# Second level of the 7-for-8 algorithm for all seven outer products of the last block's last product

## Chip, cores, metric

One core of a Trainium2 chip. The metric is the device time of one execution in microseconds (us), the median over runs.

## The reference

Attention with normalised q and k, then a bilinear feed-forward. The change touches the last line's second product only.

```python
# q, k, v: (8, 12, 448, 64); x: (3584, 768) after the heads are laid side by side
def _moe_ref(x, w_a, w_b, w_out):          # w_a, w_b: (768, 1536); w_out: (1536, 768)
    a = x @ w_a
    b = x @ w_b
    return (a * b @ w_out).astype(np.float32)
```

## The kernel before

The 3584 rows are taken in four blocks of 896 (`NB` is 4). Each block has two stages after attention: quarter products (`x @ w_a`, `x @ w_b`) and the last product (`@ w_out`). In both, a product of 2 x 2 quarters is done with seven products for eight; these seven are "product 0" to "product 6", issued in the order 0, 1, 2, 4, 3, 5, 6. In the last product, a product can be done plainly, tile by tile (128 tokens x 768 rows x 384 columns: six matmuls), or a pair of tiles can be split by the same scheme again: seven inner products of three matmuls with 192 columns each. That is the second level. It needs sums of the left factor's quarters (`Si`, four per pair, VectorE), sums of the right factor's quarters (`ti`, made once in an earlier block, kept in DRAM and fetched, four tiles per product), and more additions.

```python
        TWICE = {NB - 2: (0, 1, 2, 3, 4, 5, 6), NB - 1: (1, 2, 3, 4, 6)}   # block: products with a second level
        ...
            def each(f, a, base, to):
                twice = groups if f in TWICE.get(beta, ()) else []
                for t in pairs if not twice else alone:
                    product(t, f, a(t), plain(t, base, to))          # L726: 6 matmuls of 384 columns
                for g in twice:
                    inner_products(beta, key + place_of[f], f, g, a, base, to, acc, (c_, U_), out_place)
        ...   # groups is [(0, 1), (2, 3)] in the last block: no tile is left alone
            each(0, lambda t: A(0, 0, t), None, 0)
            for t in pairs:
                sum_(A(0, 0, t), A(0, 0, t), A(1, 0, t), ALU.subtract)
            each(1, n_, 0, 1)
            each(2, lambda t: A(0, 1, t), 0, (0, 0))
            for t in pairs:
                sum_(A(0, 1, t), A(0, 1, t), n_(t), ALU.subtract)
                sum_(n_(t), A(1, 0, t), A(1, 1, t), ALU.add)
            each(4, n_, 1, 0)
            ...
        # inside inner_products (L901 is its matmul); cut
            direct = base is None or (quarters and len(to) > 2)      # true for products 0 and 5 only
            product("a", a00, b_quarter(0, 0), nx0 + [st], True, False)
            product("b", s(1), b_made(1), ...)
            product("a", a01, b_quarter(1, 0), nx0 + [st], False, True)
            product("d", s(0), b_made(0), ...)
            product("g", s(2), b_made(2), ..., True, False)
            if not direct:                                            # two sums ahead of the read of g
                add(0.3, ...)                                         # L954
                add(0.55, ...)                                        # L955
            add(0.36, ... held["g"] ...)                              # L957: reads g before g goes on
            third()                                                   # "e"
            product("g", a11, b_made(3), ..., False, True)
```

A planner in the kernel orders all instructions beforehand from estimated durations.

In the profile lines, PE is TensorE, DVE VectorE, ACT ScalarE, POOL GpSimd and SP SyncE. `hT` holds the hidden rows (the left factor), `fin` sums of them and the running results, `st` the right factor; `Si` are the inner sums of the left factor, `ti` those of the right; `po` and `a`, `b`, `d`, `e`, `g`, `h` are PSUM banks, `pi` partial results, `oi` and `o_sb` output tiles. A line number can move by some lines in an edited kernel (L901 becomes L902).

## Time and profile before

| | |
|---|---|
| time, first three runs | 1550.15 us (1547.28 to 1551.54) |
| TensorE busy | 97%, granted clock 0.999 |
| last block's last product | 1438.38 to 1542.39, 104.0 us |
| after the last matmul | 6.2 us: one addition, then the stores |

How to read it: TensorE is never without work for long, so what shortens its queue shortens the kernel; the prediction shows the lines. The page's chain of what ended last says the same by each engine's share of the span:

```profile
PE 82%; DMA 7%; DVE 5%; ACT 3%; issue 1%; POOL 1%; SPq 1%; ACTq 0%; DVEq 0%; POOLq 0%
```

### The profile page before, as it was taken

To read this page: it belongs to the slowest core of one execution; us is meant where nothing else is said; L and a number is where in the kernel's file an instruction comes from. 1 tells how busy PE (TensorE), PEld (TensorE's weight loads), DVE (VectorE), ACT (ScalarE), POOL (GpSimd) and SP (SyncE) were. 2 spreads that over 40 slices of the span, in tenths; PEclk is the share of its full clock that TensorE was granted. 3 is DMA by queue.
4 is the path that set the end of the run, shared out by engine and by line. 5 is a ranking of instruction groups with operands and counts; after the bars stand their busy time and mean duration, and the time that the engine had idled before them with its cause. 6 is when DMAs were issued, how large, how long until landed. Compare 5 with 4: busy or idle time off the path is not lost.

```text
span 1548.6 us, 18051 instructions
## 1 busy us (share of the span) xinstructions
PE 1506.9 (97%) x6996; PEld 822.6 (53%) x6996; DVE 813.7 (53%) x1179; ACT 400.7 (26%) x654; POOL 314.1 (20%) x166
## 2 busy tenths in 40 slices
PE   8988999999999999999999999999999999999998
PEld 5553345555444555555444455555547855555796
DVE  5877869888786412222587543222237622222583
ACT  6767661111567100000445500000041000000000
POOL 3426432111345200011244300000111001000000
PEclk9999999999999999999999999999999999999999
DMA  9897445644445542212345456121226742222343
GB/s 269 240 268 199 97 108 178 218 163 175 143 118 128 150 146 76 103 71 107 102 110 152 114 159 199 72 107 71 95 83 206 247 159 100 79 82 91 111 140 110
DMA packets 128866, 214.74 MB, mean 139 GB/s; under 512 B 57860, under 2 KB 108292, under 8 KB 119044
## 3 DMA queue, kind: packets, MB, share of 16 engines
q1 hardware_dynamic: 100708, 160.02, 35.0%
q10 hardware_dynamic: 28064, 53.48, 9.9%
q8 instruction: 57, 0.93, 0.2%
q14 instruction: 37, 0.30, 0.1%
HBM read 169.08 MB, written 44.21 MB: 138 GB/s over the span
## 4 chain that ended last, share of the span: by engine, by line
PE 82%; DMA 7%; DVE 5%; ACT 3%; issue 1%; POOL 1%; SPq 1%; ACTq 0%; DVEq 0%; POOLq 0%
PE pq L1003 48%; PE po L726 16%; PE sc L515 5%; PE o L537 4%; DMA q_sb<-in_q_dram 2%; PE g L901 2%; PE a L901 2%; ACT ET L521 2%; PE pt L494 2%; DMA rec<-inv 1%; PE b L901 1%; PE su L573 1%; PE e L901 1%; PE d L901 1%; DMA lraw<-in_moe_w_b_dram 1%
## 5 line engine op out<-in xcount | busy, mean ns | idle before, releaser
L1003 PE MATMUL pq<-x,st 128*128 128x448 f32 x2016 | 763.5, 540 | 0.9 <-ACT rec L586 0.9
L1003 PEld LDWEIGHTS pq<-x,st 128*128 128x128 f32 x2016 | 381.2, 190 | 379.5 <-issue 371.2
L521 ACT ACTIVATE ET<-sc,ms 128x448 f32<-128x448 f32 x336 | 191.7, 633 | 92.2 <-PE sc L515 65.6
L515 PE MATMUL sc<-qkT 64*64 64x448 f32 x1344 | 177.2, 544 | 18.0 <-ACT ET L521 10.6
L537 PE MATMUL o<-ET,v_sb 64*64 64x448 f32 x1344 | 187.2, 545 | 7.5 <-ACT ET L521 6.9
L464 POOL TENSOR_TENSOR ms<-ms,expo 128x14 f32<-128x14 f32 x48 | 145.6, 3037 | 188.3 <-DVE ms L462 187.6
L1051 POOL TENSOR_TENSOR hT<-hT,t 128x448 f32<-128x448 f32 x24 | 28.4, 1185 | 744.7 <-DVE t L1049 742.5
L726 PE MATMUL po<-st,hT 128*128 128x384 f32 x504 | 166.4, 487 | 0.0
L726 PEld LDWEIGHTS po<-st,hT 128*128 128x128 f32 x504 | 95.0, 190 | 67.9 <-issue 3.9
L551 POOL TENSOR_TENSOR sum<-sum,ET 128x896 f32<-128x896 f32 x38 | 81.4, 2141 | 139.1 <-ACT ET L521 97.0
L1025 ACT COPY hT<-pq 128x448 f32<-128x448 f32 x24 | 12.8, 532 | 372.9 <-PE pq L1003 372.9
L515 PEld LDWEIGHTS sc<-qkT 64*64 64x64 f32 x1344 | 58.1, 132 | 95.2 <-issue 34.8
L537 PEld LDWEIGHTS o<-ET,v_sb 64*64 64x64 f32 x1344 | 60.2, 132 | 87.9 <-ACT ET L521 42.2
L726 PE MATMUL po<-st,fin 128*128 128x384 f32 x264 | 89.9, 490 | 0.0
L551 DVE TENSOR_TENSOR sum<-sum,ET 128x896 f32<-128x896 f32 x57 | 62.8, 1101 | 26.6 <-POOL sum L551 19.4
L726 PEld LDWEIGHTS po<-st,fin 128*128 128x128 f32 x264 | 49.1, 190 | 39.0 <-issue 7.0
L1063 POOL TENSOR_TENSOR hT<-hT,t 128x448 f32<-128x448 f32 x48 | 58.5, 1219 | 53.7 <-DVE t L1060 45.5
L458 DVE TENSOR_REDUCE ms<-sq 128x14 f32<-128x896 f32 x48 | 51.8, 1079 | 27.7 <-ACT sq L456 27.5
L1056 DVE TENSOR_TENSOR hT<-U,pq 128x448 f32<-128x448 f32 x48 | 29.8, 621 | 66.5 <-PE pq L1003 66.5
L746 DVE TENSOR_TENSOR o_sb<-fin,po 128x384 f32<-128x384 f32 x36 | 20.0, 554 | 80.2 <-PE po L726 72.4
L1060 DVE TENSOR_TENSOR t<-U,pq 128x448 f32<-128x448 f32 x48 | 29.7, 619 | 59.6 <-PE pq L1003 57.3
L1028 ACT COPY t<-pq 128x448 f32<-128x448 f32 x24 | 12.8, 533 | 176.0 <-PE pq L1003 176.0
(117 smaller groups left out, 1297.0 us busy)
## 6 DMA issues: line engine op xcount, KB each, us to landing
st<-kept SPq DMA_DIRECT2D x36, 1344.0 KB
st<-kept_o SPq DMA_DIRECT2D x28, 1152.0 KB
kept<-st ACTq DMA_DIRECT2D x12, 1344.0 KB
ti<-kept_t SPq DMA_DIRECT2D x48, 288.0 KB
q_sb<-in_q_dram SPq DMA_DIRECT2D x48, 224.0 KB
k_sb<-in_k_dram SPq DMA_DIRECT2D x48, 224.0 KB
v_sb<-in_v_dram SPq DMA_DIRECT2D x48, 224.0 KB
rec<-inv SPq DMA_DIRECT2D x48, 224.0 KB
```

The source lines that it names most:

```text
L458: op("DVE", 1.1, key, lambda: nc.vector.tensor_reduce(rs[p][:, s], xs["sq", nm, p], AX, ALU.add), [sq], [f"{ms}/{nm}"])
L464: lambda: nc.gpsimd.tensor_tensor(msf(), msf(), expo[:, 0:2 * NT * (b - a)], ALU.pow), [], names)
L494: nc.tensor.transpose(t[:, j * P:(j + 1) * P], x[:, j].rearrange("p h d -> p (h d)"), ident)
L515: nc.tensor.matmul(t[low_high[w], e, 0:S], lhsT=qkTs[p][low_high[e], 1, j * P + w * D:j * P + (w + 1) * D], rhs=qkTs[p][low_high[e], 0, w ...
L521: nc.scalar.activation(E[:, e], scs[p, j][:, e, 0:S], AF.Exp, scale=rs[p][:, 1, 2 * j + e:2 * j + e + 1])
L537: nc.tensor.matmul(os_[p][low_high[e], w, 0:S], lhsT=xs["v", p][low_high[w], e, j * D:(j + 1) * D], rhs=ETs[p, j][low_high[w], e], start=( ...
L551: two[e].tensor_tensor(sums[p], sums[p] if j > 1 else ETs[p, 0], ETs[p, j], ALU.add)
L726: nc.tensor.matmul(held["po"][:, 0:HALF], lhsT=a[0]()[:, c], rhs=sts[beta, 12 + place_of[f]][:, c], start=(c == 0), stop=(c == MH - 1))
L901: nc.tensor.matmul(held[bank], lhsT=x()[:, c], rhs=y(c), start=(start and c == 0), stop=(stop and c == MI - 1), skip_group_check=True)
L1003: nc.tensor.matmul(banks[bank][:, 0:S], lhsT=sts[at][:, f, c * P:(c + 1) * P], rhs=quads[x][:, c], start=(start and c == 0), stop=(stop an ...
L1056: take("DVE", 0.68, lambda bank=bank, i=i, n=n: V.tensor_tensor(C(i, n), held["U"], PS(bank), ALU.add), [f"p{ident_}.{bank}", U], [hp[i]])
L1063: lambda i=i, n=n, nm=nm: two[TIMES].tensor_tensor(C(i, n), C(i, n), held[nm], ALU.mult), [t], [hp[i]],
```

## The change

The two products that the kernel before leaves plain in the last block, 0 and 5, get the second level too: fewer matmul columns, for more sums and fetches.

```diff
-        TWICE = {NB - 2: (0, 1, 2, 3, 4, 5, 6), NB - 1: (1, 2, 3, 4, 6)}
+        TWICE = {NB - 2: (0, 1, 2, 3, 4, 5, 6), NB - 1: (0, 1, 2, 3, 4, 5, 6)}
```

## The prediction

> **What bounds the kernel now.** I read the page's head first (who is busy), then the timeline of TensorE over the last block's last product (the stage that the change touches), then the table of stretches for that stage, then the waits inside it, and last the same stage of the block before, where all seven outer products already use the second level.
>
> ```profile
> span 1548.6 us, 18051 instructions
> PE 1506.9 (97%) x6996; PEld 822.6 (53%) x6996; DVE 813.7 (53%) x1179; ACT 400.7 (26%) x654; POOL 314.1 (20%) x166
> PEclk9999999999999999999999999999999999999999
> ...
> 1438.38 11.77 PE L726 MATMUL po<-st,hT 128*128 128x384 f32 x36
> 1449.99 4.03 PE L726 MATMUL po<-st,fin 128*128 128x384 f32 x12
> 1453.86 1.14 PE L901 MATMUL a<-st,fin 128*128 128x192 f32 x6
> 1454.83 1.14 PE L901 MATMUL b<-ti,Si 128*128 128x192 f32 x6
> ...
> 1459.82 1.24 PE L901 MATMUL g<-ti,fin 128*128 128x192 f32 x6
> 1460.89 1.14 PE L901 MATMUL a<-st,fin 128*128 128x192 f32 x6
> ...
> 1485.24 1.24 PE L901 MATMUL b<-ti,Si 128*128 128x192 f32 x6 [1.80 <-DVE Si L877]
> ...
> 1512.50 11.77 PE L726 MATMUL po<-st,hT 128*128 128x384 f32 x36
> 1524.11 4.03 PE L726 MATMUL po<-st,fin 128*128 128x384 f32 x12
> 1527.98 1.14 PE L901 MATMUL a<-st,hT 128*128 128x192 f32 x6
> 1529.26 1.24 PE L901 MATMUL b<-ti,Si 128*128 128x192 f32 x6
> ```
>
> TensorE is 97% busy at full clock, and in this stage it has almost no gap, so the stage is as long as its matmuls. The stage runs from 1438.38 to 1542.40. Its seven outer products stand in the order 0, 1, 2, 4, 3, 5, 6. The two plain ones, 0 and 5, are the L726 rows: 48 instructions in 15.48 us each (1438.38 to 1453.86, 1512.50 to 1527.98), so 0.3225 us per instruction. The other five are L901: an inner product of six instructions comes every 0.975 us (1454.83 less 1453.86), 0.1625 us per instruction. A busy figure would mislead, as ends overlap; I go by start-to-start distances.
>
> ```profile
> 1438.38:1453.86 15.48, 15.48 (x50) 9.12 (x48) 9.07 (x16) 1.43 (x3) 1.13 (x1) 1.00 0.23 78
> 1453.86:1467.93 14.07, 14.07 (x85) 13.59 (x84) 9.11 (x22) 1.12 (x3) 0.00 (x0) 1.00 0.44 136
> ...
> 1482.30:1498.43 16.13, 14.33 (x85) 13.56 (x85) 13.77 (x32) 0.64 (x2) 0.00 (x0) 1.00 0.38 130
> ...
> 1512.50:1527.98 15.48, 15.48 (x50) 9.12 (x49) 4.57 (x10) 0.00 (x0) 0.00 (x0) 1.00 0.54 169
> ```
>
> The columns are length, PE, PEld, DVE, ACT, POOL, clock, DMA share and GB/s. A plain product is 15.48 us long, a two-level one 14.07 when nothing is late. VectorE and the DMA engines have room in both plain ones.
>
> **What the Trainium skill says.** "TensorE: Matmul & The Clock Gate", section "Wait — 56ns, not 53.3ns?", puts warm matmuls start to start at N / 2.4 GHz plus about 2.5 ns: 82.5 ns for 192 columns, 162.5 for 384. The trace has 162.5 and 322.5 ns, twice that within 2%, as if each f32 instruction passed its columns twice; so time follows columns, and halving them costs no visible extra here. "VectorE: DVE Perf Modes", section "The TRN2 errata", gives (N+151)/0.96 for an fp32 tensor_tensor: 557 ns for 384, 357 for 192; the trace has 554 and about 352, so it agrees. "SBUF — State Buffer", section "Who interferes with whom", says that a VectorE instruction with two SBUF inputs contends with a GpSimd instruction that reads SBUF. In the block before, one such 384-wide sum beside a GpSimd multiply took 1.49 us in place of 0.55, which fits.
>
> **The change part by part.** A plain product handles four token tiles with 4 x 6 matmuls of 384 columns, each two instructions: 48. Two-level, they go as two groups of two tiles; a group is 7 inner products of 3 matmuls of 192 columns: 42 instructions. A group therefore costs at least 7 x 0.975 = 6.83 us against 24 x 0.3225 = 7.74 us. The four new groups can give at most 4 x 0.91 = 3.7 us: the whole prize is 0.24% of the time.
> Groups seen now take 7.03 (1453.86 to 1460.89), 0.2 over 6.83: the last inner product adds into a bank that VectorE must first read, and that read comes after two sums of 0.36 and 0.56 with the earlier accumulator. Products 0 and 5 take the code's direct form, which does not put those two sums ahead. Product 5 of the block before shows it:
>
> ```profile
> 1233.57 1.14 PE L901 MATMUL g<-ti,Si 128*128 128x192 f32 x6
> 1234.55 1.14 PE L901 MATMUL e<-st,Si 128*128 128x192 f32 x6
> 1235.52 1.14 PE L901 MATMUL g<-ti,hT 128*128 128x192 f32 x6
> ```
>
> No gap before the last g, so I use 6.83 for direct groups.
> - Product 0: 15.48 becomes 2 x 6.83 + 0.1 for restarting after a wait = 13.75; saves 1.7.
> - Product 5: 15.48 becomes 13.65 + 0.15; saves 1.7.
> - Product 6 starts now with a hole: its a at 1527.98, its b only at 1529.26, 1.28 later in place of 0.975, because b needs the PSUM bank that VectorE is still reading twice for product 5. Two-level product 5 reads its banks in 0.35 us pieces, so this 0.3 goes.
> - VectorE gains, per group, four sums of 0.554 and five additions of 0.352 = 4.0 us, and in product 5 four more of 0.556 (total 6.2, against 6.83 of TensorE). It loses eight additions of 0.55 in product 5; ScalarE's four copies of 0.48 in product 0 become eight of 0.32. Net some 16 us more of VectorE work, all beside matmuls if it is in time.
> - DMA gains 8 loads of 288 KB, 2.3 MB. The block before moved 280 GB/s in one product, so about 8 us of transfer, estimated, in stretches with shares 0.23 to 0.54. The first four can be fetched during the quarter products, into the buffers that product 2's now take then; product 2's own are to be fetched in the 14 us of product 1. The factors themselves are already made for all seven.
> Sum: 1.7 + 1.7 + 0.3 = 3.7 us gained on the path, before new waits. Nothing changes after the last product (6.2 us of additions and stores), which moves earlier whole.
>
> **The rivals.**
> (1) A wait at the start of product 0 takes its place. Its sums need the last of the hidden rows; no plain tile stands in front, as one does in the block before. Product a needs no sum; b needs two. In the trace the additions that finish the rows run at 1436.33 and 1438.65 on VectorE, GpSimd's multiply for the needed rows ends at 1438.16. If the first sum slips in between (as it does in the block before), the second ends near 1439.95, and b could start at 1440.0 in place of 1439.36: 0.65 late. If the scheduler puts d, which needs one sum, ahead of b, the wait is nil; working through its rule by hand, I get a, d, b, a, which speaks for nil. With both sums after the second addition it would be 1.1. Against a large loss: product 4 has the worst such wait and it is 1.8.
> (2) VectorE becomes the bound around product 5. At 6.2 of 6.83 us it is 91% full, and the tail of product 5's second group (2.9 us) plus the sums of product 6's second group (2.2) plus product 6's own additions (3.0) make 8.1 us in a 7.03 us group. The sums are not needed until the next group, so I expect 0 to 0.5 of lateness at product 6's bank read. That whoever tuned this left out exactly the two direct products speaks for this or (1). The 1.5 us stall in product 6 of the block before looks like this rival, but VectorE waits there for a store to release its buffer, and nine such buffers are free in the last block.
> (3) Loads late: product 2's at 2.3 MB (with its factors) in about 14 us need 164 GB/s; 280 was reached. I give it little; it would cost 1 to 3 us.
> If (1) and (2) both come in full, the gain shrinks to about 2; with (3) too, the time stays where it is or rises by 1. If none comes, it is 1546.4.
>
> **Range and chances.** I take 0.8 us off the 3.7 for (1) and (2), so 2.9 us: 1550.15 - 2.9 = 1547.2. The three runs of before alone spread over 4.3 us, more than the gain, so the range is set by that spread as much as by the rivals: 1544.6 to 1549.9. Leaving the 2% band would take 31 us, eight times the whole prize: within 2% 0.985, slower 0.01 (a stuck load or a disturbed run), faster 0.005.
>
> **What would show each step right or wrong.** In the changed kernel the timeline should have no L726 rows for the last block; its products 0 and 5 should be about 13.7 to 14.3 us long; a direct group 6.83 to 6.95. The stage from its first product to the last matmul should be 100.3 to 101.6 us in place of 104.0. VectorE's busy time should rise by about 16 us. Rival 1 is a wait on the Si sums of L877 before the first b; rival 2 a wait on L957 before a g in product 5 or 6, with VectorE without idle time there; rival 3 a wait on ti or st. Wrong would be: a direct group over 7.1 us, product 4's wait grown well past 1.8 us by the longer queue on VectorE, or the schedule of the quarter products altered, which I take to be untouched.

## The result, and the profile after

Six runs each: 1544.53 us (1542.72 to 1547.83) against 1549.8 us for the kernel before. The ratio, 0.9971 with a 95% interval of 0.9957 to 0.9985, is the mean time of one kernel's fast runs over that of the other's of the same rounds, so not quite the ratio of the two medians. The time is within 2%, as expected; the median lies 0.07 us under the low end of the predicted range.

The page's head and TensorE's timeline of the stage, for the kernel after:

```profile
span 1544.2 us, 18272 instructions
PE 1503.3 (97%) x7068; PEld 832.2 (54%) x7068; DVE 824.4 (53%) x1215; ACT 401.9 (26%) x658; POOL 314.6 (20%) x166
...
1437.78 1.14 PE L901 MATMUL a<-st,hT 128*128 128x192 f32 x6
1439.19 1.24 PE L901 MATMUL b<-ti,Si 128*128 128x192 f32 x6 [0.28 <-DVE Si L877]
...
1445.15 1.14 PE L901 MATMUL a<-st,hT 128*128 128x192 f32 x6
...
1451.97 1.14 PE L901 MATMUL a<-st,fin 128*128 128x192 f32 x6
...
1483.33 1.24 PE L901 MATMUL b<-ti,Si 128*128 128x192 f32 x6 [1.80 <-DVE Si L877]
...
1510.59 1.14 PE L901 MATMUL a<-st,hT 128*128 128x192 f32 x6
...
1517.41 1.14 PE L901 MATMUL a<-st,hT 128*128 128x192 f32 x6
...
1524.24 1.14 PE L901 MATMUL a<-st,hT 128*128 128x192 f32 x6
1525.21 1.14 PE L901 MATMUL b<-ti,Si 128*128 128x192 f32 x6
...
1537.10 1.14 PE L901 MATMUL h<-ti,hT 128*128 128x192 f32 x6
```

There is no L726 row left in the stage. Product 0 goes from 1437.78 to 1451.97: 7.37 us for its first group, in which b starts 1.41 after a in place of 0.975, and 6.82 for its second. Product 5 goes from 1510.59 to 1524.24: 6.82 and 6.83. Product 6's b follows its a after 0.97, so the hole of before is gone. Product 4 waits 1.80 as it did. The stage ends at 1538.24 (1537.10 and 1.14) and takes 100.46 us. In the kernel before, the last row was

```profile
1541.25 1.14 PE L901 MATMUL h<-ti,hT 128*128 128x192 f32 x6
```

Where the 4.4 us between the two profiled spans (1548.6 and 1544.2) lie, from the two timelines:

| part | before | after | gain |
|---|---|---|---|
| up to the last product of the block before | 1170.48 | 1170.72 | -0.24 |
| last product of the block before | 78.48 | 77.64 | 0.84 |
| last block's quarter products | 189.42 | 189.42 | 0.00 |
| last block's last product | 104.01 | 100.46 | 3.55 |
| after the last matmul | 6.21 | 5.96 | 0.25 |

The first 0.60 us come before any matmul, addition or copy that the change adds or removes. Up to there it only alters which products' inner factors eight early fetches bring; the experiments come back to these fetches.

### The profile page after: what moved, and what is told of

Read it like the earlier page. It is cut to its first block, busy times and chain, and to the rows that moved or that the text cites. A ratio compares the mean times of both kernels' runs of the same rounds, so it can differ in the third digit from the quotient of the medians.

```text
span 1544.2 us, 18272 instructions
## 1 busy us (share of the span) xinstructions
PE 1503.3 (97%) x7068; PEld 832.2 (54%) x7068; DVE 824.4 (53%) x1215; ACT 401.9 (26%) x658; POOL 314.6 (20%) x166
## 4 chain that ended last, share of the span: by engine, by line
PE 83%; DMA 7%; ACT 3%; DVE 3%; issue 1%; POOL 1%; SPq 1%; ACTq 0%; DVEq 0%; POOLq 0%
PE pq L1003 49%; PE po L726 14%; PE sc L515 5%; PE o L537 5%; PE g L901 2%; PE a L901 2%; ACT ET L521 2%; DMA q_sb<-in_q_dram 2%; PE pt L494 2%; DMA kept_o<-st 2%; PE b L901 1%; PE su L573 1%; PE d L901 1%; PE e L901 1%; DMA k_sb<-in_k_dram 1%
## 5 line engine op out<-in xcount | busy, mean ns | idle before, releaser
L515 PE MATMUL sc<-qkT 64*64 64x448 f32 x1344 | 177.0, 544 | 18.6 <-ACT ET L521 10.7
L726 PE MATMUL po<-st,hT 128*128 128x384 f32 x432 | 142.9, 487 | 0.0
L726 PEld LDWEIGHTS po<-st,hT 128*128 128x128 f32 x432 | 81.3, 190 | 58.5 <-issue 3.4
L726 PE MATMUL po<-st,fin 128*128 128x384 f32 x240 | 81.8, 491 | 0.0
L726 PEld LDWEIGHTS po<-st,fin 128*128 128x128 f32 x240 | 44.6, 190 | 35.8 <-issue 7.8
```

The source lines that it names most:

```text
L515: nc.tensor.matmul(t[low_high[w], e, 0:S], lhsT=qkTs[p][low_high[e], 1, j * P + w * D:j * P + (w + 1) * D], rhs=qkTs[p][low_high[e], 0, w ...
L726: nc.tensor.matmul(held["po"][:, 0:HALF], lhsT=a[0]()[:, c], rhs=sts[beta, 12 + place_of[f]][:, c], start=(c == 0), stop=(c == MH - 1))
```

## The experiments

Every kernel gave the right result. The stage lengths, read from each profile as above, are the main evidence: those of one schedule repeat to 0.05 us, while times spread by over 1 us.

| kernel | last block's last product | the block before's | time, median |
|---|---|---|---|
| before | 104.01 | 78.48 | 1549.8 (the result's) |
| after | 100.46 | 77.64 | 1544.53 |
| after, again | 100.49 | 78.36 | 1546.1 |
| product 0 alone | 102.71 | 78.60 | 1548.57 |
| product 5 alone | 101.78 | 78.66 | 1544.57 |
| none in the last block | 108.52 | 76.92 | 1551.55 |
| after, d first | 99.94 | 78.80 | 1543.82 |
| after, 2 before 1 | 99.93 | 78.53 | 1541.52 |
| after, 2 idle sums | 100.49 | 78.14 | 1544.33 (1 run) |
| after, 5 idle sums | 100.58 | 78.35 | 1547.62 (1 run) |
| after, late loads | 100.49 | 76.91 | 1542.53 |
| 2 before 1, late differences | 99.25 | 78.63 | 1542.52 |
| all that helped | 99.43 | 76.59 | 1539.49 |
| all but d first | 98.99 | 76.59 | 1542.1 |

The kernel before ran beside the experiments with medians of 1547.77 (up to "none in the last block"), 1546.51 (up to the idle sums), 1546.92 (up to "all that helped") and 1548.51 us. Kernels are compared only within the same rounds. "All that helped" has d first, 2 before 1, late differences and late loads. "Late loads" and the last two kernels fetch the last block's inner factors late, "none" does not fetch them; all others fetch them as early as the kernel after.

### Product 0 alone, product 5 alone, none, and the change again

My theory: the gain is matmul columns less waits, all inside the stage. The rival: part of the 4.5 us is a steady gain elsewhere.

```diff
-NB - 1: (0, 1, 2, 3, 4, 5, 6)}
+NB - 1: (0, 1, 2, 3, 4, 6)}        # product 0 alone
+NB - 1: (1, 2, 3, 4, 5, 6)}        # product 5 alone
+NB - 1: ()}                        # none
```

> Second level added for product 0 alone. Theory (the gain is matmul columns, minus waits): product 0 takes 14.2 us in place of 15.48, with the same 0.3 us wait of its first b for the Si sums as in the changed kernel; product 5 stays plain at 15.48 and the hole of 0.3 us before product 6's first b stays. The stage from its first product's start to the last matmul's end is 102.7 to 102.9 us (104.0 before), the time 1.3 us shorter, a ratio of 0.9992. Rival (something outside the stage gives part of the 4.5 us): the stage as above, but the time more than 2 us shorter, a ratio under 0.9985.

> Second level added for product 5 alone. Theory: product 5 takes 13.65 us in place of 15.48, and product 6's first b follows its a after 0.975 us in place of 1.28, because the PSUM bank is free earlier; product 0 stays at 15.48. The stage is 101.7 to 101.9 us, the time 2.1 to 2.3 us shorter, a ratio of 0.9986. Rival (VectorE at 91% in product 5 costs something): a group of product 5 or the first of product 6 over 7.2 us, with a wait on L957, and the stage over 102.3. Together with the run for product 0 alone the two stage gains should add up to the 3.5 us of the whole change if the parts do not act on each other.

> No second level at all in the last block (the five products of the kernel before made plain too), a larger step in the same coin. Theory (time follows columns): each of the seven products takes 15.48 us, 108.4 us for the stage with no wait on Si sums anywhere, product 4's 1.8 us included; so 4.3 us longer than before, a ratio of 1.0028. Rival (the second level's gain is largely eaten by waits and loads): the stage under 106 us, the time within 2 us of before.

> The changed kernel once more, unedited, for more runs. Theory: the whole gain is the 3.5 us of the stage, so over these runs the ratio is 0.9977, and the 0.9971 measured first was that plus run-to-run spread of about 1 us that comes from loads and stores of earlier stages. Rival: a steady further gain of about 1 us outside the stage, so 0.9970 again. In the profile the stage should repeat to 0.2 us (100.4), and its start may differ by 1 us or more from 1437.8.

Measured, product 0 alone: stage 102.71, 1.30 shorter; first group 7.37 with the wait of 0.28 on the Si sums; ratio 0.9997 (0.9984 to 1.0011). Product 5 alone: stage 101.78, 2.23 shorter; ratio 0.9978 (0.9966 to 0.9991). The two stage gains add up to 3.53, the whole change has 3.55: the parts do not act on each other. In product 5 alone, TensorE's timeline shows the hole closed:

```profile
1524.39 1.14 PE L901 MATMUL a<-st,hT 128*128 128x192 f32 x6
1525.36 1.14 PE L901 MATMUL b<-ti,Si 128*128 128x192 f32 x6
```

None: stage 108.52, no wait in it, 4.51 longer than before (expected 4.3); ratio 1.0031 (1.0018 to 1.0044).
Again: stage 100.49, the same; ratio 0.9991 (0.9978 to 1.0003). So a steady 0.9970 did not repeat; the theory's own 0.9977 lies just outside this interval too. Over both sets, eleven runs, the changed kernel's mean is 3.2 us under the kernel before's (4.47 over six runs, 1.70 over five), which fits the stage's 3.5; what lay above it in the first set was spread. The interval for product 0 alone is too wide to see its 1.3 us in time; its stage shows it.

What I had not expected: without any second level in the last block, the last product of the block **before** takes 76.92 us, in all other kernels of this call 78.4 to 78.7. I return to it below.

### The late start of product 0

```diff
+            ahead = beta == NB - 1 and f == 0 and group[0] == 0
+            if ahead:
+                product("d", s(0), b_made(0), ...)
             product("b", s(1), b_made(1), ...)
             ...
-            product("d", s(0), b_made(0), ...)
+            if not ahead:
+                product("d", s(0), b_made(0), ...)
```

> The changed kernel with inner product d issued ahead of b in the first group of product 0. In the changed kernel the order is a, b, a, d (every such matmul writes one common token, so the scheduler keeps the order of the code, which the prediction overlooked), and the first b comes 0.43 us late behind the Si sums. d needs only the first sum, which is ready before a starts. Theory: with a, d, b, a the wait is nil, the first group takes 6.83 to 6.95 us in place of 7.37 and the stage 100.0 in place of 100.46; in time 0.4 us, not to be seen in the spread. Rival (the late start is another thing, such as the PSUM bank of the quarter product before): b or d still starts late, the group stays over 7.2.

Measured: stage 99.94, first group 6.83, no wait (ratio 0.9976, 0.9954 to 0.9997). TensorE's timeline of that kernel:

```profile
1435.45 1.14 PE L901 MATMUL a<-st,hT 128*128 128x192 f32 x6
1436.42 1.14 PE L901 MATMUL d<-ti,Si 128*128 128x192 f32 x6
1437.40 1.14 PE L901 MATMUL b<-ti,Si 128*128 128x192 f32 x6
```

So the loss in product 0 was the order b before d: 0.54 us of the group (7.37 to 6.83), 0.5 us of stage.

### How near VectorE is to the bound in product 5

```diff
+            for _ in range(2 if beta == NB - 1 and f == 5 else 0):      # and 5 in the other run
+                add(0.43, lambda: V.tensor_tensor(<unused columns of S>, held["t"][:, 0:256], held["t"][:, 0:256], ALU.add), ...)
```

> How near VectorE is to being the bound in product 5: two sums of 256 columns that serve nothing are added to each of its two groups, some 0.4 us each (estimated from 0.35 for 192 and 0.55 for 384 columns), so 7.05 us of VectorE work in a group of 6.83. Theory (there is slack, as sums are made a group ahead): products 5 and 6 lengthen by under 0.3 us, from 27.65 to at most 27.95. Rival (it is at the edge): they lengthen by 0.5 us or more, with waits on L957.

> Five such sums in each group of product 5: 8.3 us of VectorE work in a group of 6.83. Both theories expect a loss here: VectorE is over by some 3 us in two groups, less the lead it has. Theory (lead of about one group's sums, 2.2 us): products 5 and 6 lengthen by 0.5 to 2 us. Rival (no lead): by 2.5 us or more. Under 0.3 would say that VectorE is nowhere near the bound and that its busy sum misleads.

Measured: with two sums per group products 5 and 6 do not change (6.82, 6.83, 7.02, 6.99; stage 100.49), with five the second group becomes 6.91 and the stage 100.58. Under 0.3 both times: for two sums my expectation held; for five, both theories expected a loss of 0.5 us or more, and both missed. So rival 2 of the prediction is out, and my working of it was wrong. VectorE's timeline with five idle sums shows why:

```profile
1510.84 0.35 DVE L971 TENSOR_TENSOR oi<-pi,e 128x192 f32<-128x192 f32 x1
1511.10 0.55 DVE L877 TENSOR_TENSOR Si<-Si,hT 128x384 f32<-128x384 f32 x1
1511.57 0.35 DVE L976 TENSOR_TENSOR oi<-pi,g 128x192 f32<-128x192 f32 x1
1511.84 0.55 DVE L877 TENSOR_TENSOR Si<-hT,fin 128x384 f32<-128x384 f32 x1
...
1513.95 2.26 DVE L938 TENSOR_TENSOR Si<-pi 128x256 f32<-128x256 f32 x5
1516.13 0.35 DVE L947 TENSOR_TENSOR pi<-pi,d 128x192 f32<-128x192 f32 x1
```

The second column is the time that one lasts, the first its start. A sum of 384 columns lasts 0.55 us, but the next starts after 0.47; one of 192 lasts 0.35 and holds the engine for 0.27. I had added up durations: 8 x 0.555 + 5 x 0.352 = 6.2 us for a group of product 5. By starts it is 8 x 0.47 + 5 x 0.27 = 5.1, 75% of 6.83. That is a lower bound: where the next sum needs a tile of the one before, it starts later (L976 at 1518.77, L978 at 1519.36 in the changed kernel, 0.59). That kernel's second group of product 5, which has these 13 instructions, shows VectorE busy for 5.52 us, 81%. The five idle sums take 2.18 (1513.95 to 1516.13), which makes 7.3 to 7.7, over 6.83 by 0.5 to 0.9 in each of two groups. Sums are made a group ahead; that this lead takes up the rest is argued, not shown.

### Product 4's wait

Not part of the change, but the largest wait left in the stage: 1.8 us before and after.

```diff
-for f in (0, 1, 2, 4, 3, 5, 6):                       # and place_of to match
+for f in (0, 2, 1, 4, 3, 5, 6):
-            each(1, n_, 0, 1)
             each(2, lambda t: A(0, 1, t), 0, (0, 0))
             for t in pairs:
                 sum_(A(0, 1, t), A(0, 1, t), n_(t), ALU.subtract)
+            each(1, n_, 0, 1)
+            for t in pairs:
                 sum_(n_(t), A(1, 0, t), A(1, 1, t), ALU.add)
```

> The changed kernel with product 2 before product 1 in the order. Product 4 waits 1.8 us for sums that can be made only after product 2 (a difference for product 3) and product 1 (the reuse of the N tiles); with 2 first, these sums spread over two products. Theory (the wait is VectorE's queue at that one place): product 4's first group takes 7.0 to 7.9 in place of 9.1 us, the stage 98.5 to 99.4 us, the time 1 to 2 us shorter than that of the changed kernel. Rival (VectorE is simply short of time in this whole stretch): the wait moves to another group, and the stage stays within 0.4 us of 100.5.

Measured: stage 99.93, 0.53 shorter. Product 4's groups take 7.03 and 7.03, but the wait has moved: product 1's first group takes 8.71. Neither theory had it whole. TensorE, then VectorE, of that kernel:

```profile
1461.44 1.14 PE L902 MATMUL a<-st,fin 128*128 128x192 f32 x6
1463.98 1.24 PE L902 MATMUL b<-ti,Si 128*128 128x192 f32 x6 [1.40 <-DVE Si L878]
...
1460.23 0.95 DVE L714 TENSOR_TENSOR hT<-hT,fin 128x768 f32<-128x768 f32 x1
...
1461.92 0.95 DVE L714 TENSOR_TENSOR fin<-fin 128x768 f32<-128x768 f32 x1
1462.78 0.55 DVE L878 TENSOR_TENSOR Si<-fin 128x384 f32<-128x384 f32 x1
```

The Si sums, for which TensorE waits, stand behind L714's 768-wide sums, which later products need. So I gave the differences written over the hidden rows (for products 5 and 3) a lower priority:

```diff
-                op("DVE", 0.98, -0.5, lambda: ...)
+                op("DVE", 0.98, key, lambda: ...)      # key -0.2 for product 5's, -0.45 for product 3's, else -0.5
```

> Product 2 before product 1 as in the run before this one, and in addition the in-place differences of the hidden rows (needed by products 5 and 3) at a lower priority than the Si sums. With the swap alone the wait moved to product 1's first group (8.71 us, 1.40 on Si sums), 0.5 us won. Theory (the wait is the order of VectorE's queue: sums that are needed late stand ahead of sums that are needed now): no group over 7.6 us, the stage 98.6 to 99.3. Rival (VectorE has too much work in the first three products): a wait of over 1 us stays somewhere before product 3, the stage 99.7 or more.

Measured: stage 99.25, the longest group outside product 0 7.42; ratio 0.9963 (0.9946 to 0.9979). The wait was the order of VectorE's queue, for the larger part: with both edits the stage is 1.2 us shorter than the changed kernel's. The lower priority without the swap was not run. Several groups are now some 0.3 us longer than 7.03, with waits on L958 (the read of g), so VectorE's work there is not without cost.

### The block before, and what its stalls come from

In the block before, the split pair of product 5 or of product 6, or both, stalls by 0.2 to 2.0 us, in all kernels told so far but the one without second level in the last block. There the 7 buffers of the last block's inputs leave two for output tiles, and a tile waits until an earlier store has landed. In the kernel before, VectorE, then TensorE:

```profile
1242.59 0.35 DVE L936 TENSOR_TENSOR pi<-pi,b 128x192 f32<-128x192 f32 x1 [1.47 <-PE b L901]
1245.78 0.35 DVE L942 TENSOR_TENSOR oi<-fin,a 128x192 f32<-128x192 f32 x1 [2.83 <-DMA out_dram<-oi]
...
1247.88 1.24 PE L901 MATMUL g<-ti,hT 128*128 128x192 f32 x6 [1.50 <-DVE oi L957]
```

In this stretch all kernels but that one already fetch the inner factors of the last block's first two products, eight tiles of 288 KB, some 190 us or more before they are used. I delayed these fetches:

```diff
-               [f"kt{f}.{n}.0", f"kt{f}.{n}.{MI - 1}", "ended"]
+               [f"kt{f}.{n}.0", f"kt{f}.{n}.{MI - 1}", "ended"] + ([f"h{beta}/1"] if beta == NB - 1 else [])
```

> The changed kernel with the inner factors of the last block fetched later: not in the last product of the block before, as soon as their buffers are free, but once the second row of that last block's quarter products is done. In the run without second level in the last block, which has none of these loads, the last product of the block before took 76.9 us; in all others 77.6 to 78.8, with product 5 or 6 waiting for the store of an output tile to free its buffer. Theory (these loads, a block early, hold up the stores): that stage takes 76.9 to 77.1 us, the last block's stage stays 100.5, and the time is 0.7 to 1.8 us shorter than that of the changed kernel, a ratio to before of 0.996 to 0.9975. Rival (the stores are slow by themselves, and the one quick run was chance): that stage stays at 77.6 to 78.8.

Measured: 76.91 us for that stage, 100.49 for the last; ratio 0.9971 (0.9955 to 0.9988). The same place in that kernel, VectorE, then TensorE:

```profile
1237.43 0.35 DVE L936 TENSOR_TENSOR pi<-pi,b 128x192 f32<-128x192 f32 x1 [1.47 <-PE b L901]
1238.34 0.35 DVE L942 TENSOR_TENSOR oi<-fin,a 128x192 f32<-128x192 f32 x1 [0.55 <-PE a L901]
...
1241.15 1.24 PE L901 MATMUL g<-ti,hT 128*128 128x192 f32 x6
```

The early fetches hold up the stores, and the stores hold up TensorE, by an amount that differs from run to run: 77.64 to 78.80 us in the eight profiles with products 1 and 2 in the old order and early fetches. The 0.84 us of the first pair of profiles lie within this spread: before and after both have eight fetches there (of products 1 and 2 before, of 0 and 1 after), and the changed kernel profiled again has 78.36, near the 78.48 of the kernel before. So they are most likely not the change's doing; the kernel before has only one profile here. The late part comes after the issue: SyncE issues product 5's stores 66.92 us after the stage's start in the kernel before (1237.40) and with late fetches (1232.24), but they free the buffer at 75.30 (1245.78) in the one and by 73.02 (1238.34) in the other. Whether they are held in the queue that they share with the fetches or on the DMA engines was not told apart.

### All together

> Everything that helped together: all seven products on the second level, d ahead of b in the first group, product 2 before product 1, the in-place differences at lower priority, the inner factors fetched late. If the parts add up: last block's stage 98.2 to 98.9 us, the block before 76.9 to 77.1, time 3 to 4 us shorter than the changed kernel and 6.5 to 7.5 us shorter than before, a ratio of 0.9953. Rival (they take from each other, as VectorE's queue is shared): the last block's stage over 99.3, ratio over 0.9965.

Measured: 1539.49 us, ratio 0.9944 (0.9929 to 0.9959), the kernel with the lowest ratio: its mean is 8.0 us under that of the kernel before, where the change alone has 3.2. The block before takes 76.59, the last block's stage 99.43, which misses the 98.2 to 98.9 expected and is over the rival's 99.3, though the ratio is under the rival's 0.9965: the parts take from each other, as product 2's second group now takes 7.84. To tell whether d first or the late fetches did that, I ran the same kernel without d first.

> The run with everything together, less d ahead of b. In that run product 2's second group took 7.84 us with a wait of 0.53 on Si sums; in the run without d first and without late fetches it took 7.03. If d first causes it: the group is 7.0 to 7.1 here, product 0's first group is 7.37 again, the last block's stage 99.0 to 99.3. If the late fetches cause it: the group stays near 7.8 and the stage is about 99.9. The block before takes 76.5 to 76.7 either way, and the time is within 1 us of the run with everything.

Measured: that group 7.03, product 0's first 7.37, stage 98.99, the block before 76.59; ratio 0.9953 (0.9940 to 0.9966), 6.7 us in means. So d first causes it: it gives 0.54 at the start and takes back nearly 1.0 in product 2's two groups (7.18 and 7.84 against 7.03 and 7.03). VectorE's timelines show how: the planner orders its queue anew, and with d first five 768-wide sums (L714) stand ahead of the first Si sum of product 2's second group, which starts 21.30 us after the stage's start (1454.98); without d first four do, and it starts at 17.82 (1452.26). TensorE, with d first:

```profile
1456.18 1.24 PE L902 MATMUL b<-ti,Si 128*128 128x192 f32 x6 [0.53 <-DVE Si L878]
```

By the stages this kernel should be 0.4 us the faster of the two; the times have it slower by more than that (medians 2.6 us apart where I had expected 1 at most, ratios 0.9953 and 0.9944), with intervals that overlap, so which of the two is better stays open. They were run at other times. Both beat the kernel before in time. That they beat the changed one too is shown by the stages; the times fit it. Against the second profile of the change the two stages of this last kernel are 1.50 and 1.77 shorter, 3.3 us together, which agrees with the 6.7 less 3.2 in the times.

## Why the prediction was right or wrong

- **TensorE bounds the stage, time follows columns.** Right. Direct groups take 6.82 to 6.83 us against the 6.83 worked out, and without any second level the stage grows by 4.51 us.
- **Product 0, 13.75.** It took 14.19. The failed step: "working through its rule by hand, I get a, d, b, a". I overlooked that the common token keeps TensorE in the order of the code, which is a, b, a, d. So the first rival came, 0.43 us of the 0.65 that the prediction gave for it; the experiment with d first removed it, though combined with the other edits that costs more later than it gives.
- **Product 5, 13.8.** It took 13.65; the 0.15 of margin was not needed.
- **Product 6's hole of 0.3.** Right: 1.28 became 0.97, and in product 5 alone too.
- **VectorE, "91% full", 8.1 us in a 7.03 us group.** Mis-sized: durations overlap their successors, and product 5's group is 75% full by starts, 81% by the profile's busy time. Busy time rose by 10.7 us, not 16, for the 36 more instructions that the parts give. The reading of "SBUF — State Buffer", section "Who interferes with whom" (the Trainium skill), fits the changed kernel too: a 384-wide sum that started beside a GpSimd multiply took 1.49 us in place of 0.55. The multiply, which had itself started beside an earlier sum, took 1.38 in place of 1.13.
- **Loads.** Right as far as the new ones go: no wait on ti or st appears in the stage. The early fetches hurt a block earlier, and did so before the change as well.
- **The sum.** 3.7 less 0.8 was predicted, 3.55 measured in the stage. Of the 0.8 set aside for the rivals 0.43 came, and product 5 and product 6's hole gave some 0.15 and 0.1 more than their terms. The first six runs gave 4.5, five more 1.7, so the time alone could not have judged the steps.

## What to carry to other kernels

When an engine is 97% busy, count its instructions by start-to-start distances in the stage that changes, and read the new stage's length from the timeline; here a gain of 0.2% repeated to 0.05 us there and was nearly lost in the spread of times. Before hand-simulating a scheduler, look for tokens that every instruction of an engine writes. Fetching early is not free: eight tiles fetched 190 us ahead held up stores that a busy engine was waiting for.

## What the Trainium skill lacked or had wrong

- "VectorE: DVE Perf Modes", section "The DRAIN you can't avoid", says that an instruction which is not held starts before the pipe of the one ahead is empty, and this section has no figure for it (the figure is missing there, not in the whole skill). Here fp32 sums of 384 columns last 0.55 us and follow each other after 0.47, or after 0.59 where the next needs a tile of the one before; those of 192 last 0.35 and hold the engine for 0.27. So added durations overstate VectorE's load: 6.2 us for a group of product 5, against 5.1 by starts and 5.52 by busy time.
- "TensorE: Matmul & The Clock Gate", section "Wait — 56ns, not 53.3ns?", gives the distance of matmuls without a word on f32 operands in that section (other pages of the skill do speak of fp32). Here an f32 instruction of 192 columns takes 162.5 ns and one of 384 takes 322.5, about twice the figure, and each matmul of the code is two instructions.
